# Order of score maxima, low parts of q and weight steps, PSUM bank order and idle matmuls in a fused attention and two-MLP kernel on one core

## The chip, the core and the metric

One Trainium2 chip, one of its cores. The metric is the device time of one execution in microseconds (us), the median of the runs shown. TensorE (PE) does the matmuls and has a queue of its own for weight loads (PEld); VectorE (DVE), ScalarE (ACT) and GpSimd (POOL) work on elements; SyncE's queue (SP) issues the DMAs. Each engine runs its own instructions in the order in which the program lists them, and waits on semaphores for what the others make.

## The reference

Batch 2, 12 heads, 448 positions, head size 64, all float32. Cut to what matters:

```python
scores = (q @ k.T) / 8                       # per head, 448 x 448
scores = where(upper triangle, -1e9, scores) # causal
p = exp(scores - max(scores))
attn = p / (sum(p) + 1e-9)
x = (attn @ v) -> 896 tokens x 768
y = (sigmoid(x @ w_gate) * (x @ w_val)) @ w_out        # d_ff 1536
h = y @ w_in                                           # 1024
s = h * softmax(h)
out = (layernorm(s) * g_ln) @ w_out2                   # 896 x 768
```

## The kernel before, in words

**Numbers.** A float32 operand of a matmul is split in two: a *high* part, which is the operand rounded to the type that PE takes, and a *low* part, which is what is left. A product is three matmuls: high by high, high by low, low by high (`TERMS`). So each operand costs two instructions outside PE, the low part after the high part. The weights come from memory as 64-bit words and are first turned into float32 by bit operations.

**Attention in pairs of heads.** The 24 heads are 12 pairs, `p` = 0 to 11. For one pair:

- q and k are loaded (`load_qk`, tile `qkr`); POOL makes k's and q's high parts (L223 and L236; for pair 0 DVE does it, since `prep_q_hi` is called with another engine there), DVE makes k's low part (`prep_k_lo`, L231) and q's low part (`prep_q_lo`, L253), all into one tile `qks`.
- The queries lie in four tiles of 64, 128, 128 and 128 rows that need 64, 192, 320 and 448 keys (`QE`). They are worked in two groups, `GROUPS` = tiles (3, 0) with 448 and 64 keys, and tiles (2, 1) with 320 and 192. A group's scores, for both heads of the pair, share one tile `s` of two PSUM banks, from the pool `ps_s`, which holds two such tiles. PE first writes the mask with bf16 matmuls (`sc_mask`, L341), then adds the scores (`sc_dots`, L354): for each query tile three times two matmuls, q's high part by k's high part, q high by k low, q low by k high.
- DVE takes the maxima (`sc_max`, L368), one instruction for each query tile and both heads, into the small tile `sum0`, `sum1` or `sum2` (the pairs in turn); ACT takes the exponentials (`sc_exp`, L375) into the tile `p`, one instruction for each query tile and head, and adds up the row sums.
- The probabilities are transposed by PE, in two units for each head (`tr_mm`, L426, tile `t`, pool `ps_t`); ACT makes the high part (`tr_hi`, L433), DVE the low part (`tr_lo`, L231), both into a tile `pt`. PE multiplies with v (`pv_mm`, L458, tile `x`, pool `ps_x`); v's two parts are made by POOL (`prep_v_hi`, L223; `prep_v_lo`, L231).
- The row sums' reciprocals (`recips`, L384) are spread by POOL and PE (`rs_wide`, `rs_mm`), copied by ACT (`rs_out`), and DVE multiplies the result (`x_mul`, L464). `x_hi` and `x_lo` split it for the next stage.

**The order.** It is written out by hand: a software pipeline of steps `s`, eight to a pair (`PER`). The table `STEPS` (L504) says for each function at which step, counted from the pair's own start at step 8p, it is issued, on which engine, and for which pairs (two further numbers, from and below). At each step the loop (L533) issues what is due, first on PE, then ACT, DVE, POOL; on one engine the order within a step is that of the table, and for a function with a negative step it is done ahead of the pair's start. So a row `(-8, 'D', prep_q_lo, 2)` puts q's low part of pairs from 2 on at the step at which the pair before starts. SP's queue holds the loads, issued where `prep_k_lo`, `prep_v_lo` and the weights' steps stand; pair 2's q and k are loaded behind pair 0's low parts.

**Idle matmuls.** `keep_warm` (L317, matmuls at L319, tile `warm`) issues bf16 matmuls whose result nobody reads: 56 at the front, 24 each at steps 2, 5 and 9.

**The weights' first chunks.** From step 88 the loop also prepares chunks of the first MLP's weights, one chunk `c` after another: an ACT scaling (L114) and three DVE steps (L117, L119, L122, the last one also issues the next chunk's load), then the high part on ACT (`chunk_hi`, L133) and the low part on DVE (`chunk_lo`, L136). Behind pair 11's start PE takes matmuls of the first MLP (`gv`) between the attention's (`early_tiles`, L478, matmuls at L490), in a PSUM tile of the pool `ps_s`; ACT copies them out (`pre`, L495).

**The next stages.** Then all PSUM banks go to one pool, and PE runs the first MLP's `gv` (L597), `pm` (L627), the second MLP's `h` (L657) and `po` (L718). A tile of the new pool waits for what last used its bank. The attention's pools take their banks in the order in which they are opened: `ps_s` the lowest four, then `ps_t` two, then `ps_x` two.

## Time and profile before

| | |
|---|---|
| median of 3 runs | 508.43 us (508.19 to 508.91) |
| the profiled execution | 507.66 us, its span 505.9 us |
| PE busy | 494.8 us, 98% of the span |
| DVE, ACT, POOL busy | 334.2, 224.5, 119.8 us (66%, 44%, 24%) |
| granted PE clock | 1.00 over the span |

The span runs from the first instruction to the last; the execution's own time also holds what lies around it. The attention takes about the first 122 us, the first MLP the time to some 378 us, the second one the rest. Two other facts help with the rows further below: "L354" is line 354 of the kernel before, and a bracket such as [1.30 <-DVE pt L231] gives the idle time of the engine just before the instruction, and the instruction that ended it. A row with a count, as x12, is a run of alike instructions and gives the start of the first and the time from it to the end of the last.

### The profile page before, as it was taken

Reading aid. Unit: us, or ns where it says so; the run is one execution under the profiler, and the core shown is the slowest. Engines: PE = TensorE matmul, PEld = TensorE weight load, DVE = VectorE, ACT = ScalarE, POOL = GpSimd, SP = SyncE. Lnnn points to the kernel's source line nnn. Section 1 sums busy time; section 2 is a strip of 40 time slices with the busy share of each in tenths; the row PEclk is TensorE's granted clock in tenths of the full one; section 3 lists DMA queues with packets and bytes.
Section 4 is the critical chain, followed back from the end, with each engine's and each line's share of the span. In section 5 each row is a group of like instructions: output and inputs, shape, how many; then the busy total and the mean of one; then the engine's idle time right before and its main releaser. Section 6 shows DMA issues by size and latency. Waiting matters only on the chain.

```text
span 505.9 us, 7924 instructions
## 1 busy us (share of the span) xinstructions
PE 494.8 (98%) x3076; PEld 455.0 (90%) x3076; DVE 334.2 (66%) x514; ACT 224.5 (44%) x481; POOL 119.8 (24%) x207
## 2 busy tenths in 40 slices
PE   8899999999999999999999999999999999999997
PEld 8789998988999999999999999999998888899997
DVE  6778787886576677778877676776664787831110
ACT  4687878765424434543454333334313242422211
POOL 4667676641000000000000000000060597710000
PEclk9999999999999999999999999999999999999999
DMA  5724242023323433454443323335530311000101
GB/s 152 235 64 104 69 109 65 23 64 125 112 76 126 134 127 118 163 166 128 164 166 122 134 100 131 113 132 166 183 129 0 123 66 63 1 32 34 60 32 62
DMA packets 13205, 52.81 MB, mean 104 GB/s; under 512 B 1776, under 2 KB 2288, under 8 KB 13168
## 3 DMA queue, kind: packets, MB, share of 16 engines
q1 hardware_dynamic: 13168, 52.31, 31.7%
q8 instruction: 24, 0.39, 0.3%
q14 instruction: 13, 0.11, 0.1%
HBM read 49.55 MB, written 2.75 MB: 103 GB/s over the span
## 4 chain that ended last, share of the span: by engine, by line
PE 78%; ACT 11%; DVE 6%; issue 2%; DMA 1%; POOL 0%; SPq 0%; DVEq 0%; POOLq 0%; ACTq 0%
PE gv L597 33%; PE pm L627 17%; PE po L718 12%; PE h L657 12%; ACT p L375 7%; ACT pt L433 3%; DVE sum L368 2%; DVE qks L253 2%; PE gv L490 2%; DMA qkr<-in_qk_dram 1%; PE tp L700 1%; PE x L458 1%; DVE pt L231 1%; PE t L426 1%; DVE rs L384 0%
## 5 line engine op out<-in xcount | busy, mean ns | idle before, releaser
L597 PE MATMUL gv<-xy,hl 128*128 128x448 f32 x828 | 168.1, 365 | 0.6 <-ACT pre L495 0.6
L597 PEld LDWEIGHTS gv<-xy,hl 128*128 128x128 f32 x828 | 155.4, 188 | 13.3 <-ACT pre L495 1.0
L627 PE MATMUL pm<-g,hl 128*128 128x448 f32 x432 | 87.7, 365 | 0.0
L627 PEld LDWEIGHTS pm<-g,hl 128*128 128x128 f32 x432 | 81.1, 188 | 6.4
L644 POOL TENSOR_SCALAR t<-t,g_sb 128x768 f32<-128x768 f32 x8 | 8.8, 1102 | 249.1 <-PE pm L627 248.1
L136 DVE TENSOR_TENSOR hl<-t,hl 128x768 fp32r<-128x768 f32 x36 | 34.8, 967 | 41.3 <-ACT hl L133 39.6
L718 PE MATMUL po<-wo,lt 128*128 128x384 f32 x336 | 60.6, 339 | 0.0
L657 PE MATMUL h<-wi,xy 128*128 128x512 f32 x252 | 59.2, 395 | 0.0
L718 PEld LDWEIGHTS po<-wo,lt 128*128 128x128 f32 x336 | 58.7, 188 | 0.1
L657 PEld LDWEIGHTS h<-wi,xy 128*128 128x128 f32 x252 | 47.2, 187 | 11.4
L375 ACT ACTIVATE p<-s,sum 128x448 f32<-128x448 f32 (+3 forms) x96 | 45.9, 499 | 25.2 <-DVE rs L384 17.8
L122 DVE SCALAR_TENSOR_TENSOR t<-raw,t 128x768 int32<-128x768 int32 (+1 forms) x56 | 53.0, 946 | 1.7
L119 DVE SCALAR_TENSOR_TENSOR t<-raw,t 128x768 int32<-128x768 int32 (+1 forms) x56 | 52.8, 943 | 1.8
L114 ACT ACTIVATE raw<-raw 128x768 f32<-128x768 f32 (+1 forms) x56 | 47.9, 865 | 10.6 <-DMA raw<-in_wo_dram 7.9
L458 PE MATMUL x<-pt,v 128*128 128x320 f32 (+3 forms) x252 | 51.1, 323 | 0.0
L231 DVE TENSOR_TENSOR pt<-t,pt 128x512 fp32r<-128x512 f32 (+1 forms) x48 | 32.3, 672 | 19.2 <-ACT pt L433 19.2
L458 PEld LDWEIGHTS x<-pt,v 128*128 128x128 f32 x252 | 38.9, 190 | 1.9
L117 DVE TENSOR_SCALAR t<-raw 128x768 int32<-128x768 int32 (+1 forms) x56 | 30.9, 552 | 4.7 <-ACT raw L114 4.7
L173 DVE TENSOR_TENSOR lt<-tp,lt 128x512 fp32r<-128x512 f32 x14 | 9.7, 690 | 36.4 <-ACT lt L172 36.4
L133 ACT CAST hl<-t 128x768 fp32r<-128x768 f32 x36 | 30.0, 832 | 4.8 <-PE pm L627 4.2
L368 DVE TENSOR_REDUCE sum<-s 128x2 f32<-128x896 f32 (+3 forms) x48 | 30.2, 668 | 2.0 <-PE s L354 2.0
L181 ACT ACTIVATE wk<-gv 128x448 f32<-128x448 f32 x23 | 11.3, 542 | 44.2 <-PE gv L597 44.2
(95 smaller groups left out, 550.9 us busy)
## 6 DMA issues: line engine op xcount, KB each, us to landing
raw<-in_gv_dram SPq DMA_DIRECT2D x24, 768.0 KB, 4.5
raw<-in_wo_dram SPq DMA_DIRECT2D x20, 768.0 KB, 4.5
raw<-in_wi_dram SPq DMA_DIRECT2D x12, 512.0 KB, 3.5
qkr<-in_qk_dram SPq DMA_DIRECT2D x22, 224.0 KB, 3.8
vr<-in_v_dram SPq DMA_DIRECT2D x12, 256.0 KB, 2.8
out_dram<-o SPq DMA_DIRECT2D x6, 384.0 KB, 2.3
qkr<-in_qk_dram SPq DMA_DIRECT2D x4, 112.0 KB, 2.7
out_dram<-o SPq DMA_DIRECT2D x2, 192.0 KB, 1.9
```

Source lines behind the costliest of these rows:

```text
L114: nc.scalar.activation(out=w1.bitcast(F32), in_=w1.bitcast(F32), func=AF.Copy, scale=2.0 ** -112)
L119: nc.vector.scalar_tensor_tensor(out=tt, in0=w1, scalar=-2 ** 31, in1=tt, op0=ALU.bitwise_and, op1=ALU.bitwise_or)
L122: nc.vector.scalar_tensor_tensor(out=tt, in0=w0, scalar=29, in1=tt, op0=ALU.logical_shift_right, op1=ALU.bitwise_or)
L136: nc.vector.tensor_tensor(out=lo, in0=t_t.pop(it), in1=f32(hi), op=ALU.subtract)
L231: (nc.gpsimd if eng == 'P' else nc.vector).tensor_tensor(out=out, in0=a, in1=b, op=ALU.subtract)
L368: nc.vector.reduce_max(out=sum_t[p % 3][:, 8 + 2 * i:10 + 2 * i], in_=ps_sc[p, i], axis=AX.X, negate=True)
L375: nc.scalar.activation(out=p_t[(2 * p + e) % NPB][:, POFF[i]:POFF[i] + n], in_=ps[:, 1 - e], func=AF.Exp, bias=mx, scale=1.0, accum_out=sm)
L458: nc.tensor.matmul(out=ps[:, 128 * j:], lhsT=l, rhs=pt_t[h][:, c, u, c0:c0 + S - 128 * j], start=(chunk == 0 and n == 0), stop=(chunk == 7 ...
L597: nc.tensor.matmul(out=ps[i, b], lhsT=w[:, a, cs], rhs=xy[kk][:, x, b * S:(b + 1) * S], start=(kk == 0 and a == 0 and x == 0), stop=(kk == ...
L627: nc.tensor.matmul(out=ps[b], lhsT=w[:, a, cs], rhs=g_t[kk][:, x, b * S:(b + 1) * S], start=(kk == 0 and a == 0 and x == 0), stop=(kk == N ...
L657: nc.tensor.matmul(out=h[:, n * 512:(n + 1) * 512], lhsT=xy[kk][:, a, tk], rhs=wi[n * NK + kk][:, c], start=(kk == 0 and i == 0), stop=(kk ...
L718: nc.tensor.matmul(out=ps[n], lhsT=lts[k // 4][:, a, k % 4], rhs=wo[k][:, c, cs], start=(k == 0 and i == 0), stop=(k == NF2 - 1 and i == 2))
```

## The change

It consists of six edits, and none alters what is computed.

1. The PSUM pools are opened in another order: `ps_t` has the lowest two banks, `ps_x` the next two, `ps_s` the highest four.
2. Idle matmuls: 44 instead of 56 at the front; instead of 24 each at steps 2, 5 and 9, there are 20 at step 8 and 8 at step 9.
3. For pair 0, group 0, the maxima are four instructions, one for each head and query tile, head by head, and the exponentials of both query tiles are issued in one step, head by head too.
4. Pair 0's scores of both groups are issued at step 0 (group 1's were at step 4), and its maxima of group 1 at step 1. Pair 1 keeps its groups at steps 0 and 4.
5. q's low part moves: for pair 1 from step -2 to step -5, ahead of k's low part; for pairs from 2 on from step -8 to step -7. At step -8 it was issued ahead of the maxima of group 0 of the pair before, at step -7 it stands behind them.
6. The weights' chunks take 8 steps each instead of 9, and within a chunk the steps stand at 0, 3, 5 and 7 (before 0, 2, 4 and 6), ahead of the high part at 8 and the low part at 9 (before 7 and 8).

```diff
--- before.py
+++ after.py
@@ -196,9 +196,9 @@
         ptp = actx.enter_context(tc.tile_pool(name="ptp", bufs=4, side="right"))
         st = actx.enter_context(tc.tile_pool(name="st", bufs=2, side="right"))
         xfp = actx.enter_context(tc.tile_pool(name="xfp", bufs=2, side="right"))
-        ps_s = actx.enter_context(tc.tile_pool(name="ps_s", bufs=2, space=PSUM, reuse_waits="tile"))
         ps_t = actx.enter_context(tc.tile_pool(name="ps_t", bufs=2, space=PSUM, reuse_waits="tile"))
         ps_x = actx.enter_context(tc.tile_pool(name="ps_x", bufs=2, space=PSUM, reuse_waits="tile"))
+        ps_s = actx.enter_context(tc.tile_pool(name="ps_s", bufs=2, space=PSUM, reuse_waits="tile"))
 
         NH = B * H
         qk_raw, qk_sp = {}, {}
@@ -318,7 +318,7 @@
             for _ in range(n):
                 nc.tensor.matmul(out=ps[:, :128], lhsT=identb, rhs=identb, start=True, stop=True)
 
-        keep_warm(56)
+        keep_warm(44)
         prep_k_hi(0)
         prep_k_lo(0)
         prep_q_hi(0, 'D')
@@ -364,16 +364,22 @@
             return sum_t[p % 3][:, k:k + 1], sum_t[p % 3][:, m:m + 1]
 
         def sc_max(p, g):
-            for i in GROUPS[g]:
-                nc.vector.reduce_max(out=sum_t[p % 3][:, 8 + 2 * i:10 + 2 * i], in_=ps_sc[p, i], axis=AX.X, negate=True)
-
-        def sc_exp(p, i):
-            n = QE[i]
-            ps = ps_sc.pop((p, i))
-            for e in range(2):
+            if p == 0 and g == 0:
+                for e in range(2):
+                    for i in GROUPS[g]:
+                        nc.vector.reduce_max(out=sums_of(p, i, e)[1], in_=ps_sc[p, i][:, 1 - e], axis=AX.X, negate=True)
+            else:
+                for i in GROUPS[g]:
+                    nc.vector.reduce_max(out=sum_t[p % 3][:, 8 + 2 * i:10 + 2 * i], in_=ps_sc[p, i], axis=AX.X,
+                                         negate=True)
+
+        def sc_exp(p, *tiles):
+            for e, i in ([(e, i) for e in range(2) for i in tiles] if p == 0 else
+                         [(e, i) for i in tiles for e in range(2)]):
+                n = QE[i]
                 sm, mx = sums_of(p, i, e)
-                nc.scalar.activation(out=p_t[(2 * p + e) % NPB][:, POFF[i]:POFF[i] + n], in_=ps[:, 1 - e], func=AF.Exp,
-                                     bias=mx, scale=1.0, accum_out=sm)
+                nc.scalar.activation(out=p_t[(2 * p + e) % NPB][:, POFF[i]:POFF[i] + n], in_=ps_sc[p, i][:, 1 - e],
+                                     func=AF.Exp, bias=mx, scale=1.0, accum_out=sm)
 
         def sums(p):
             rs = rs_t[p] = st.tile([128, 16], F32, tag="rs", name="rs")
@@ -500,26 +506,25 @@
         early = early_tiles()
         left = NE * 6 * NK
 
-        ONE = 2
         STEPS = (
-            (0, 'E', lambda p: sc_mm(p, (0, 1) if p >= ONE else (0,))),
-            (4, 'E', lambda p: sc_mm(p, () if p >= ONE else (1,))),
+            (0, 'E', lambda p: sc_mm(p, (0,) if p == 1 else (0, 1))), (4, 'E', lambda p: sc_mm(p, (1,)), 1, 2),
             *((s0 + d, eng, lambda p, f=f, u=u, a=a: f(2 * p + a, u))
               for u, a, s0 in ((1, 0, 9), (1, 1, 11), (0, 0, 13), (0, 1, 15))
               for d, eng, f in ((0, 'E', tr_mm), (1, 'A', tr_hi), (1 if s0 == 15 else 2, 'D', tr_lo))),
             *((13 + n, 'E', lambda p, n=n: pv_mm(p, n)) for n in range(len(CHUNKS))),
             (15, 'E', rs_mm),
-            (-7, 'P', prep_k_hi, 0, 2), (-6, 'P', prep_q_hi, 0, 2), (-2, 'D', prep_q_lo, 0, 2),
+            (-7, 'P', prep_k_hi, 0, 2), (-6, 'P', prep_q_hi, 0, 2), (-5, 'D', prep_q_lo, 0, 2),
             (-5, 'D', prep_k_lo, 0, 2),
-            (-10, 'P', prep_k_hi, 2), (-9, 'P', prep_q_hi, 2), (-8, 'D', prep_q_lo, 2), (-2, 'D', prep_k_lo, 2),
+            (-10, 'P', prep_k_hi, 2), (-9, 'P', prep_q_hi, 2), (-7, 'D', prep_q_lo, 2), (-2, 'D', prep_k_lo, 2),
             (3, ENG['lk'], last_keys), (7, ENG['vh'], prep_v_hi), (9, ENG['vl'], prep_v_lo),
             (8, 'P', sums), (9, 'D', recips), (10, ENG['rx'], rs_wide), (16, ENG['rr'], rs_out),
             (21, 'D', x_mul), (24, ENG['xh'], x_hi, 0, NPR - 1), (25, ENG['xl'], x_lo, 0, NPR - 1),
             (22, ENG['xh'], x_hi, NPR - 1), (23, ENG['xl'], x_lo, NPR - 1),
-            (1, 'A', lambda p: sc_exp(p, 3)), (2, 'A', lambda p: sc_exp(p, 0)),
+            (1, 'A', lambda p: sc_exp(p, 3, 0), 0, 1), (1, 'A', lambda p: sc_exp(p, 3), 1),
+            (2, 'A', lambda p: sc_exp(p, 0), 1),
             (5, 'A', lambda p: sc_exp(p, 2)), (6, 'A', lambda p: sc_exp(p, 1)),
-            (0, 'D', lambda p: sc_max(p, 0)),
-            (2, 'D', lambda p: sc_max(p, 1), ONE), (4, 'D', lambda p: sc_max(p, 1), 0, ONE),
+            (0, 'D', lambda p: sc_max(p, 0)), (1, 'D', lambda p: sc_max(p, 1), 0, 1),
+            (4, 'D', lambda p: sc_max(p, 1), 1, 2), (2, 'D', lambda p: sc_max(p, 1), 2),
         )
 
         def steps(s, eng):
@@ -531,8 +536,8 @@
 
 
         for s in range(PER * NPR + 26):
-            if s in (2, 5, 9):
-                keep_warm(24)
+            if s in (8, 9):
+                keep_warm(20 if s == 8 else 8)
             steps(s, 'E')
             for _ in range(2):
                 if s >= PER * NPR and left and next(early):
@@ -544,15 +549,16 @@
                 dma_next()
 
             for c in range(2 * NE + 2):
-                e = s - 88 - 9 * c
+                e = s - 88 - 8 * c
+                if e in (3, 5, 7):
+                    next(bits_now)
+                if e == 8 and c < 2 * NE:
+                    chunk_hi(c)
+                if e == 9 and c < 2 * NE:
+                    chunk_lo(c)
                 if e == 0:
                     bits_now = bits_steps(c)
-                if e in (0, 2, 4, 6):
                     next(bits_now)
-                if e == 7 and c < 2 * NE:
-                    chunk_hi(c)
-                if e == 8 and c < 2 * NE:
-                    chunk_lo(c)
         while left:
             left -= next(early)
         for t in range(NE):
```

In the diffs of the order below, names carry the number of their buffer, `out<-in`; the line numbers of the changed kernel are higher by up to 6.

**DVE, the first two pairs.** In DVE's list from the low part of pair 0's q on, before: `s_249` and `s_308` are pair 0's two groups of scores, `s_365` is pair 1's first, `qks_274` is pair 1's q and k, `qks_360` pair 2's.

```order
L253 SCALAR_TENSOR_TENSOR qks_241<-qkr_110,qks_241 128x448
L368 TENSOR_REDUCE sum0_157<-s_249 128x2 x2
L231 TENSOR_TENSOR qks_274<-qkr_115,qks_274 128x448
L368 TENSOR_REDUCE sum0_157<-s_308 128x2 x2
L253 SCALAR_TENSOR_TENSOR qks_274<-qkr_115,qks_274 128x448
L253 SCALAR_TENSOR_TENSOR qks_360<-qkr_246,qks_360 128x448
L368 TENSOR_REDUCE sum1_158<-s_365 128x2 x2
L384 RECIPROCAL rs_389<-rs_389 128x8
```

And now (`s_237` and `s_258` pair 0's scores, `s_327` pair 1's first, `qks_289` pair 1's, `qks_302` pair 2's):

```order
L253 SCALAR_TENSOR_TENSOR qks_229<-qkr_110,qks_229 128x448
L370 TENSOR_REDUCE sum0_157<-s_237 128x1 x4
L373 TENSOR_REDUCE sum0_157<-s_258 128x2 x2
L253 SCALAR_TENSOR_TENSOR qks_289<-qkr_115,qks_289 128x448
L231 TENSOR_TENSOR qks_289<-qkr_115,qks_289 128x448
L373 TENSOR_REDUCE sum1_158<-s_327 128x2 x2
L253 SCALAR_TENSOR_TENSOR qks_302<-qkr_234,qks_302 128x448
L390 RECIPROCAL rs_350<-rs_350 128x8
```

Pair 0's two groups of maxima now follow each other, and pair 1's first maxima stand ahead of pair 2's q low part, where they stood behind it.

**DVE, a later pair.** One pair's turn from one transposes' low part to the next, before (`s_649` and `s_670` are the pair's two groups, `qks_629` the next pair's q and k):

```order
L231 TENSOR_TENSOR pt_603<-t_631,pt_603 128x512
L253 SCALAR_TENSOR_TENSOR qks_629<-qkr_489,qks_629 128x448
L368 TENSOR_REDUCE sum0_157<-s_649 128x2 x2
L384 RECIPROCAL rs_702<-rs_702 128x8
L368 TENSOR_REDUCE sum0_157<-s_670 128x2 x2
L231 TENSOR_TENSOR pt_720<-t_704,pt_720 128x512
```

And now, with `s_595` and `s_616` in their places and `qks_575` as the next pair's:

```order
L231 TENSOR_TENSOR pt_549<-t_577,pt_549 128x512
L373 TENSOR_REDUCE sum0_157<-s_595 128x2 x2
L253 SCALAR_TENSOR_TENSOR qks_575<-qkr_435,qks_575 128x448
L390 RECIPROCAL rs_647<-rs_647 128x8
L373 TENSOR_REDUCE sum0_157<-s_616 128x2 x2
L231 TENSOR_TENSOR pt_666<-t_649,pt_666 128x512
```

q's low part has moved from ahead of the first group's maxima to behind them, and stays ahead of the reciprocals and of the second group's maxima.

**DVE, the last pair.** From the last maxima on, before (`raw_391` is the first chunk of weights):

```order
L368 TENSOR_REDUCE sum2_159<-s_1773 128x2 x2
L117 TENSOR_SCALAR t_1830<-raw_391 128x768
L231 TENSOR_TENSOR pt_1822<-t_1807,pt_1822 128x512
L119 SCALAR_TENSOR_TENSOR t_1830<-raw_391,t_1830 128x768
L231 TENSOR_TENSOR pt_1846<-t_1832,pt_1846 128x512
L464 TENSOR_TENSOR xf_1861<-x_1719,rb_1798 128x448
L122 SCALAR_TENSOR_TENSOR t_1830<-raw_391,t_1830 128x768
L231 TENSOR_TENSOR pt_1822<-t_1849,pt_1822 128x448
```

And now (`raw_352` is the first chunk):

```order
L373 TENSOR_REDUCE sum2_159<-s_1719 128x2 x2
L231 TENSOR_TENSOR pt_1768<-t_1753,pt_1768 128x512
L117 TENSOR_SCALAR t_1786<-raw_352 128x768
L231 TENSOR_TENSOR pt_1792<-t_1776,pt_1792 128x512
L470 TENSOR_TENSOR xf_1806<-x_1665,rb_1744 128x448
L119 SCALAR_TENSOR_TENSOR t_1786<-raw_352,t_1786 128x768
L231 TENSOR_TENSOR pt_1768<-t_1794,pt_1768 128x448
L122 SCALAR_TENSOR_TENSOR t_1786<-raw_352,t_1786 128x768
```

Each step of the first chunk of weights has moved behind the transposes' low part that it stood ahead of.

## Rows read from the trace of the kernel before

**Rows 1.** The chain that ended last, its shares of the span by engine.

```profile
PE 78%; ACT 11%; DVE 6%; issue 2%; DMA 1%; POOL 0%; SPq 0%; DVEq 0%; POOLq 0%; ACTq 0%
```

**Rows 2.** Windows: length, busy us of PE, PEld, DVE, ACT, POOL, PEclk, DMA, GB/s.

```profile
10.00:20.00 10.00, 8.23 (x114) 7.49 (x113) 7.05 (x12) 6.72 (x29) 6.59 (x14) 1.00 0.65 230
...
130.00:290.00 160.00, 160.00 (x791) 148.28 (x790) 116.60 (x162) 66.59 (x103) 0.00 (x0) 1.00 0.39 131
```

**Rows 3.** PE's waits over the span: what for, us, times, longest.

```profile
PE t L426 <- DVE pt L231: 4.5, 12, 1.3
...
PE gv L597 <- ACT pre L495: 0.6, 1, 0.6
PE gv L490 <- DVE hl L136: 0.6, 1, 0.6
```

**Rows 4.** The chain that ended last, near the start: start us, us, what.

```profile
6.01 0.64 DVE qks L253
7.22 4.42 DMA qkr<-in_qk_dram
...
12.38 0.54 POOL qks L236
12.94 0.91 DVE qks L253
13.85 1.21 DVE sum L368 x2
```

**Rows 5.** PE's timeline: start us, us from first to last, engine, line, instruction.

```profile
1.61 4.68 PE L319 MATMUL warm<-identb 128*128 128x128 bf16 x56 [1.61 <-DVE identb L280]
...
7.44 1.51 PE L319 MATMUL warm<-identb 128*128 128x128 bf16 x24
...
11.65 1.11 PE L354 MATMUL s<-qks 64*128 64x448 f32 x12
...
17.74 0.33 PE L426 MATMUL t<-identx,p 128*128 128x128 f32 x1 [1.30 <-DVE pt L231]
...
19.62 0.30 PE L426 MATMUL t<-identx,p 128*128 128x128 f32 x1 [0.47 <-DVE pt L231]
...
27.15 0.33 PE L426 MATMUL t<-identx,p 128*128 128x128 f32 x1 [0.58 <-DVE pt L231]
...
88.75 1.11 PE L354 MATMUL s<-qks 64*128 64x448 f32 x12
...
104.08 0.33 PE L426 MATMUL t<-identx,p 128*128 128x128 f32 x1 [0.39 <-DVE pt L231]
```

**Rows 6.** Groups by form, 0 to 110 us: count, busy us, mean ns, idle before.

```profile
L368 DVE TENSOR_REDUCE sum<-s 128x2 f32<-128x896 f32 x12 | 12.9, 1079 | 1.2 <-PE s L354 1.2
...
L368 DVE TENSOR_REDUCE sum<-s 128x2 f32<-128x128 f32 x12 | 3.3, 275 | 0.0
```

**Rows 7.** DVE's timeline, columns as in rows 5.

```profile
7.55 1.29 DVE L368 TENSOR_REDUCE sum<-s 128x2 f32<-128x896 f32 x2 [0.92 <-PE s L354]
...
11.34 0.61 DVE L253 SCALAR_TENSOR_TENSOR qks<-qkr,qks 128x448 fp32r<-128x448 f32 x1
...
89.53 0.79 DVE L253 SCALAR_TENSOR_TENSOR qks<-qkr,qks 128x448 fp32r<-128x448 f32 x1
...
91.56 1.23 DVE L368 TENSOR_REDUCE sum<-s 128x2 f32<-128x640 f32 x2
...
93.49 0.69 DVE L231 TENSOR_TENSOR pt<-t,pt 128x512 fp32r<-128x512 f32 x1 [0.70 <-ACT pt L433]
...
102.14 1.27 DVE L119 SCALAR_TENSOR_TENSOR t<-raw,t 128x768 int32<-128x768 int32 x1
```

**Rows 8.** ACT's timeline, columns as in rows 5.

```profile
8.94 0.63 ACT L375 ACTIVATE p<-s,sum 128x448 f32<-128x448 f32 x1 [4.10 <-DVE sum L368]
...
10.46 0.32 ACT L375 ACTIVATE p<-s,sum 128x64 f32<-128x64 f32 x1
```

**Rows 9.** POOL's timeline, columns as in rows 5.

```profile
14.43 1.42 POOL L231 TENSOR_TENSOR v<-vr,v 128x384 fp32r<-128x384 f32 x2
```

## The prediction

> **What bounds the kernel now.** I read the page first, there the chain that ended last: PE holds 78% of it, ACT 11% and DVE 6% [rows 1]. So a saving counts only where PE waits. The windows say where that is: PE is busy 8.23 of the ten microseconds from 10 to 20 us, but 160.00 of 160 us from 130 to 290 us [rows 2]. The list of PE's waits then adds up all there is to win after the start: twelve waits for the low part of the transposed probabilities, 4.5 us in all, and two single waits of 0.6 us, for the weights' low part and for the copy `pre` [rows 3].
>
> Which work is late there is told by the chain [rows 4]. It comes from the load of pair 2's q and k, which takes until 11.64 us, through POOL's high parts and DVE's low part of q of pair 2 (12.94 us, 0.91 us), and only then do pair 1's maxima run (13.85 us). Pair 1's maxima do not need pair 2's q. They stand behind it in DVE's order, although PE had pair 1's first scores finished at 12.76 us (11.65 + 1.11) [rows 5]. From the maxima the chain goes through the exponentials to a transpose that PE starts at 17.74 us after 1.30 us of idleness; the next such wait is 0.47 us, pair 1's is 0.58 us, and one near the end 0.39 us [rows 5]. That leaves 4.5 - 1.30 - 0.47 - 0.58 - 0.39 = 1.76 us for the other eight, 0.22 us for each later pair.
>
> **The change, part by part.** All sums are against the profiled execution (span 505.9 us, its own time 507.66 us, 0.77 us under the median of 508.43 us); I carry the difference over to the median.
>
> *Start (pairs 0 and 1).* Idle matmuls: 24 take 1.51 us, 0.063 us each; the first 56 take 4.68 us, 1.15 us more than at that rate [rows 5], as if some of them ran at the lower level (1.2 GHz). Twelve fewer end the front 0.76 us earlier, at 5.5 us (1.61 + 4.68 - 0.76). Pair 0's first dots then wait for q's high part, which DVE ends just ahead of q's low part, and the third pair of matmuls waits for the low part, done at 6.65 us (6.01 + 0.64) [rows 4]; eight matmuls at the pace of the 1.11 us burst [rows 5] end at about 7.3 us, 0.2 us earlier than before.
>
> The maxima of group 0 become four reductions over one head each. None is in the trace. From the forms of 896 and 128 elements, 1.079 and 0.275 us [rows 6], one element costs 1.05 ns and an instruction 0.14 us: 0.61 us for 448, 0.21 us for 64. With the 0.07 us by which neighbours overlap, four take 1.43 us where two took 1.29 us [rows 7]. Bounds: 1.29 us (work by element alone) and 1.8 us (no overlap, and 64 elements as long as 128: 2 x (0.61 + 0.275)). I take the fit, and the maxima end at 8.76 us. Splitting them frees nothing early: the first exponential waits for all four, since they write one tile.
>
> The four exponentials took 8.94 to 10.78 us [rows 8], so now end at 10.70 us. That frees the score tile for pair 1's masks, at 10.75 us. DVE meanwhile does group 1's maxima (1.23 us), then pair 1's q low and k low (0.61 us each) [rows 7], from 8.7 until 11.1 us with the hand-overs. The third dot of pair 1 waits for that, and some 0.85 of the 1.11 us burst follows: 11.95 us. Pair 1's maxima start at 12.0 instead of 13.78 us, because pair 2's q low part (ready for POOL's sake at 12.92 us) now comes after them. **Term: -1.8 us**, between -1.4 (reductions at 1.8 us) and -2.1 us (the burst without a hitch). Exponentials, high part, low part and the transpose shift with it; the waits of 1.30 and 0.47 us stay, as they are part of that chain. Next to be late is v's low part, which POOL ends at 15.85 us (14.43 + 1.42) [rows 9]; PE would reach its first use at some 16.5 us, so it just stays hidden. The 44 other idle matmuls that vanish (2.8 us) lie in stretches where PE would wait anyway, so I cost them at nothing beyond this shift; that is true while masks wait for the exponentials.
>
> *Steady pairs.* Each period had 0.79 us of q's low part ahead of the maxima [rows 7]. It now stands between the two groups' maxima, beside ACT's exponentials of group 0. In the period that I read, q low ended at 90.32 us (89.53 + 0.79) and the maxima followed, while PE's dots of group 0 had ended at 89.86 us (88.75 + 1.11) [rows 5, 7]: they may start 0.46 us earlier. PE's wait is 0.22 us, so it goes. What is late next: between the maxima of group 0 and the transposes' low part DVE now has q low (0.61 us) besides group 1's maxima (1.23 us). There it sat idle 0.70 us until ACT was done [rows 7], and 0.61 us of that is now used. **Term: -0.58 - 1.76 = -2.3 us**, between 0 and -2.3 us.
>
> *Drain.* The first weights' steps run one step later: the short shift instead of the 1.27 us step stands ahead of a transpose's low part, so the wait of 0.39 us at 104.08 us [rows 5, 7] goes. The wait for the weights' low part (0.6 us) turns into one for the high part, which is now made later too: 0, with bounds -0.6 and +0.4 us. The other wait of 0.6 us [rows 3] ends because the transposes' banks are lowest: the first `gv` tile of the next stage then takes a bank that is long free, not the one that `pre` is copied from. **Term: -1.0 us**, between -0.6 and -1.6 us. Chunks 2 and 3 get their steps earlier by up to three steps, on engines that are then idle: 0.
>
> **Sum:** -1.8 - 2.3 - 1.0 = -5.1 us; 507.66 becomes 502.6 us, and the median 508.43 becomes **503.3 us**. With all bounds: -2.0 to -6.0 us, so 502.4 to 506.4 us. The steady bound of 0 is a case of its own, below; with the steady term kept the ends are 502.4 and 504.1 us.
>
> **Rivals.**
> 1. *The steady wait stays.* The moved q low part delays group 1's maxima and with them the transposes' low part. For it: only some 0.1 us of the 0.70 us idle time is left, and the same instruction takes 0.61 us at 11.34 us but 0.91 us at 12.94 us, where POOL works too [rows 4, 7]; at 0.91 us the margin is gone. Against it: POOL waits for the reciprocal behind it, so it runs alone. Then -1.8 - 1.0 = -2.8 us: 505.6 us, and 504.5 us if half the wait stays. The Trainium skill ("SBUF — State Buffer", Who interferes with whom) says that a VectorE instruction with two inputs in SBUF and a reading GpSimd instruction block each other for a whole instruction; by that rule a meeting would cost 0.54 us, one POOL instruction [rows 4]. The row at 12.94 us shows 0.30 us lost, so the trace agrees in kind and shows less.
> 2. *The clock falls, and the kernel is slower.* PE's granted clock is 1.00 (2.4 GHz) in all rows [rows 2], also across the pause of 1.30 us. The change takes out 56 idle matmuls and leaves longer pauses before pair 1's masks and before the first transpose (15.95 us). At 1.2 GHz PE's work takes twice as long, and the front's extra 1.15 us is what one return cost: one fall gives 504.5 us. Slower than before by 0.2% needs over 6.1 us lost, 12 us at the lower level, so six falls, or a low level through pairs 1 and 2. Against it: longer idle time with little change in busy share did not lower it before. The Trainium skill ("TensorE: Matmul & The Clock Gate", What's actually happening) says that the half rate is the default and that only activity keeps the clock up, which speaks against taking idle matmuls out; by that rule a fall costs what is priced here, and no row of this kernel shows one after the start.
> 3. *The start's shift is lost* to POOL: v's low part or pair 2's preparation, both bound by the load until 11.64 us [rows 4], hold the first product chunk, and about 1 us of the 1.8 goes: 504.3 us.
>
> **How the numbers follow.** Forecast 503.3 us (502.4 to 504.1): 0.66. Rival 1: 0.16. Rival 3: 0.08. Rival 2: 0.07, of which 0.03 ends slower than 509.4 us. Several gains being larger than rows say (overlap in the dots, the drain's -1.6 us): 0.03. Timings of this kernel spread over 0.7 us, so about 0.2% (1.0 us) can be told from no change. Faster 0.94, same 0.03, slower 0.03. The range 502.0 to 505.7 us takes in the forecast, rivals 1 and 3 and one fall of the clock; outside lie a fall that lasts and gains well beyond all bounds.
>
> **What would show it.** In the new profile pair 1's maxima start near 12.0 us, with pair 2's q low part after them; pair 2's score masks stand some 1.8 us earlier; PE's list of waits keeps about 1.3 and 0.5 us for the transposes and none of 0.2 us in later pairs; the first `gv` matmuls of the next stage follow without a wait, some 5 us earlier than now. I am wrong if the small waits come back with DVE named, if idle matmuls lie 0.11 us apart after 5 us, or if PE waits for POOL's v.

## The result, and the profile after

The changed kernel takes **501.65 us** (median of 4 runs, 501.51 to 501.92) against 508.31 us before (4 runs, 508.09 to 508.91): a ratio of 0.9868, 95% interval 0.9851 to 0.9885, so 6.7 us less. The direction was forecast. The size was not: 503.3 us was expected, and 501.65 us lies 0.35 us below the range. The profiled execution took 501.62 us, its span is 499.7 us (before 505.9 us).

The page of the profile after shows in its chain, by engine, that PE now holds nearly all of the path (78% in [rows 1]):

```profile
PE 94%; DVE 2%; ACT 2%; issue 1%; POOL 0%; POOLq 0%; DVEq 0%; ACTq 0%
```

The list of PE's waits after (what for, us in total, times, longest), beside [rows 3]:

```profile
PE t L432 <- DVE pt L231: 1.7, 2, 1.2
...
PE s L341 <- ACT p L381: 1.3, 1, 1.3
PE gv L496 <- ACT hl L133: 1.0, 1, 1.0
PE gv L496 <- ACT pre L501: 0.2, 1, 0.2
```

Ten of the twelve waits for the transposes' low part are gone, and so is the one at the entry of the next stage. New is a wait of pair 1's masks for pair 0's exponentials, in a place where idle matmuls ran before.

Where the 6.2 us of span went is read from the places at which PE starts a pair's masks or a stage. PE's timeline before (start us, us, engine, line, instruction), at the first masks of pair 2, of pair 11, and at the next stage:

```profile
21.12 0.23 PE L341 MATMUL s<-maskb,identb 64*128 64x128 bf16 x2
...
96.95 0.23 PE L341 MATMUL s<-maskb,identb 64*128 64x128 bf16 x2
...
122.92 12.43 PE L597 MATMUL gv<-xy,hl 128*128 128x448 f32 x60 [0.62 <-ACT pre L495]
```

And PE's timeline after, with the waits between:

```profile
5.75 0.23 PE L341 MATMUL s<-maskb,identb 64*128 64x128 bf16 x2
...
10.81 0.23 PE L341 MATMUL s<-maskb,identb 64*128 64x128 bf16 x2 [1.27 <-ACT p L381]
...
10.98 1.12 PE L354 MATMUL s<-qks 64*128 64x448 f32 x12
...
16.11 0.33 PE L432 MATMUL t<-identx,p 128*128 128x128 f32 x1 [1.23 <-DVE pt L231]
...
18.00 0.30 PE L432 MATMUL t<-identx,p 128*128 128x128 f32 x1 [0.47 <-DVE pt L231]
...
19.49 0.23 PE L341 MATMUL s<-maskb,identb 64*128 64x128 bf16 x2
...
91.80 0.23 PE L341 MATMUL s<-maskb,identb 64*128 64x128 bf16 x2
...
102.85 0.68 PE L496 MATMUL gv<-xy,hl 128*128 128x448 f32 x2 [0.95 <-ACT hl L133]
...
116.77 18.40 PE L603 MATMUL gv<-xy,hl 128*128 128x448 f32 x90
```

| stretch | before, us | after, us | difference | forecast |
|---|---|---|---|---|
| to pair 2's masks | 21.12 | 19.49 | -1.63 | -1.8 |
| pair 2's to pair 11's masks | 75.83 | 72.31 | -3.52 | -2.3 |
| pair 11's masks to the next stage | 25.97 | 24.97 | -1.00 | -1.0 |
| from there to the end of the span | 382.98 | 382.93 | -0.05 | 0 |

Start and drain came as forecast; the later pairs gained 1.2 us more. One such pair shows why. PE before, from six matmuls with v to a transpose that waited, and on to one that did not:

```profile
92.92 1.11 PE L458 MATMUL x<-pt,v 128*128 128x448 f32 x6
94.24 0.33 PE L426 MATMUL t<-identx,p 128*128 128x128 f32 x1 [0.21 <-DVE pt L231]
...
94.65 1.00 PE L458 MATMUL x<-pt,v 128*128 128x320 f32 x6
95.49 0.27 PE L426 MATMUL t<-identx,p 128*128 128x128 f32 x1
```

The same first two groups after:

```profile
88.11 1.11 PE L464 MATMUL x<-pt,v 128*128 128x448 f32 x6
89.09 0.33 PE L432 MATMUL t<-identx,p 128*128 128x128 f32 x1
```

The transpose that waited started 1.32 us after the six matmuls began, now it is 0.98 us: 0.34 us less, for a wait whose row says 0.21 us. The row counts from the *end* of the last matmul, which the profile models. In an unbroken stream the next matmul starts before that end: 95.49 us is 0.16 us ahead of 95.65 (94.65 + 1.00), and 89.09 is 0.13 us ahead of 89.22. So a wait cost its row and this lost overlap.

DVE's timeline after shows the moved instruction where the diff put it, behind the maxima, and the low part of the transposes behind it without a wait (before: 0.70 us of idle time, [rows 7]):

```profile
12.13 1.29 DVE L373 TENSOR_REDUCE sum<-s 128x2 f32<-128x896 f32 x2 [1.14 <-PE s L354]
13.34 0.81 DVE L253 SCALAR_TENSOR_TENSOR qks<-qkr,qks 128x448 fp32r<-128x448 f32 x1
...
86.30 0.75 DVE L253 SCALAR_TENSOR_TENSOR qks<-qkr,qks 128x448 fp32r<-128x448 f32 x1
86.97 0.19 DVE L390 RECIPROCAL rs<-rs 128x8 f32<-128x8 f32 x1
87.08 1.23 DVE L373 TENSOR_REDUCE sum<-s 128x2 f32<-128x640 f32 x2
88.35 0.69 DVE L231 TENSOR_TENSOR pt<-t,pt 128x512 fp32r<-128x512 f32 x1
```

### The profile page after: what moved, and what is told of

Its sections match the earlier page's. It is cut to its first block, busy times and chain, and to the rows that moved or that the text cites. A ratio compares the mean times of both kernels' runs of the same rounds, so it can differ in the third digit from the quotient of the medians.

```text
span 499.7 us, 7812 instructions
## 1 busy us (share of the span) xinstructions
PE 490.5 (98%) x3020; PEld 452.4 (91%) x3020; DVE 333.7 (67%) x516; ACT 224.7 (45%) x481; POOL 117.6 (24%) x207
## 4 chain that ended last, share of the span: by engine, by line
PE 94%; DVE 2%; ACT 2%; issue 1%; POOL 0%; POOLq 0%; DVEq 0%; ACTq 0%
PE gv L603 34%; PE pm L633 18%; PE po L724 12%; PE h L663 12%; PE x L464 6%; PE t L432 4%; PE s L354 4%; PE gv L496 1%; PE tp L706 1%; PE s L341 1%; PE r L404 1%; PE warm L319 1%; ACT p L381 1%; DVE pt L231 1%; DVE sum L373 0%
## 5 line engine op out<-in xcount | busy, mean ns | idle before, releaser
L373 DVE TENSOR_REDUCE sum<-s 128x2 f32<-128x640 f32 (+3 forms) x46 | 29.0, 672 | 3.6 <-PE s L354 3.6
```

## The experiments

Three theories stood against each other for the later pairs. **A:** the order of q's low part is the whole gain, and a wait costs its row and 0.13 us. **B:** a wait costs its row, the rest is another edit's. **C:** the banks carry it. The runs of the kernel before beside the experiments had medians of 508.07 to 508.41 us.

**e1, q's low part put back** in the changed kernel, pairs 3 to 11:

```diff
-(-7, 'D', prep_q_lo, 2)
+(-7, 'D', prep_q_lo, 2, 3), (-8, 'D', prep_q_lo, 3)
```

> The changed kernel (501.65 us, period of a later pair 8.03 us), with q's low part of pairs 3 to 11 put back ahead of the maxima of the pair before. Theory A: the order of q's low part is the whole gain of the later pairs, and a wait of PE costs its row and 0.13 us more, because the matmul ahead of it is no longer overlapped by the next. Then nine waits on the transposes' low part come back (about 0.5 and eight of 0.22 us), the period is 8.39 us again, and the time is 501.65 + 3.5 = 505.2 us. Theory B: a wait costs what its row shows, and the rest of the gain of the later pairs is from another edit. Then the same rows come back, but the period is 8.25 us and the time 504.0 us. Theory C: another edit (the banks) carries the later pairs. Then the period stays 8.03 us and the time 501.7 us.

505.39 us (504.96 to 505.81), ratio 0.9945 (0.993 to 0.996). PE's timeline, one period from masks to masks:

```profile
61.90 0.19 PE L341 MATMUL s<-maskb,identb 64*128 64x64 bf16 x2
...
67.45 0.33 PE L432 MATMUL t<-identx,p 128*128 128x128 f32 x1 [0.22 <-DVE pt L231]
...
70.29 0.19 PE L341 MATMUL s<-maskb,identb 64*128 64x64 bf16 x2
```

The period is 8.39 us and the row 0.22 us: 0.36 us more for 0.22 us shown. That is theory A, and B and C fall.

**e2, q's low part moved alone** in the kernel before, for pairs 3 to 11; pair 2's stays at -8.

```diff
-(-8, 'D', prep_q_lo, 2)
+(-8, 'D', prep_q_lo, 2, 3), (-7, 'D', prep_q_lo, 3)
```

> The kernel before (508.31 us, period 8.39 us), with q's low part of pairs 3 to 11 alone moved behind the maxima of the pair before; pair 2's stays where it was, and so does all else. Theory A: the period falls to 8.03 us, the nine waits after pair 2's first masks go, and the time is 508.31 - 3.5 = 504.8 us. Theory B: the waits go, the period falls to 8.17 us only, and the time is 506.0 us. Theory C: the period stays 8.39 us and the time 508.3 us.

504.57 us (504.53 to 504.62), 3.5 us under the 508.07 us beside it; ratio 0.9929 (0.9914 to 0.9944). The old banks, the old idle matmuls and the old weights' steps all stand in it. Of the waits on the transposes' low part only the two of the start and the last pair's (0.38 us) are left, and the period is 8.04 us:

```profile
45.77 0.19 PE L341 MATMUL s<-maskb,identb 64*128 64x64 bf16 x2
...
53.81 0.19 PE L341 MATMUL s<-maskb,identb 64*128 64x64 bf16 x2
```

One moved instruction is more than half of the whole gain.

**e12, q's low part twice** in its new place, to find the margin and price a longer wait:

```diff
 (-7, 'D', prep_q_lo, 2),
+(-7, 'D', prep_q_lo, 3),
```

> The changed kernel with q's low part of pairs 3 to 11 computed twice in its new place, one after the other, with the same result. The transposes' low part behind it ended 0.05 us before PE took its bank in the later pairs, so there is no margin: the period grows by the time of one more instruction, 0.54 to 0.7 us, and the time by nine times that, 501.65 + 4.9 to 6.3 us = 506.5 to 508 us. Theory A: PE's row of this wait is 0.13 us shorter than what the period grew by. Theory B: the row is as long as what the period grew by. Third reading: there was a margin of 0.3 us or more, and the period grows by less than 0.3 us, 504.4 us or less.

506.23 us (505.19 to 507.05), ratio 0.9955 (0.9936 to 0.9974).

```profile
53.92 0.19 PE L341 MATMUL s<-maskb,identb 64*128 64x64 bf16 x2
...
59.52 0.33 PE L432 MATMUL t<-identx,p 128*128 128x128 f32 x1 [0.27 <-DVE pt L231]
...
62.36 0.19 PE L341 MATMUL s<-maskb,identb 64*128 64x64 bf16 x2
```

The period grew by 0.41 us (8.44), the row shows 0.27: again 0.14 us more than the row. The second instruction adds about 0.54 us (half of the pair's 1.27 us, less the 0.1 us by which neighbours overlap), so the margin was some 0.13 us, larger than expected here. One of the nine periods is longer: there the two instructions took 1.79 us, the row shows 0.79 us and the period is 8.96 us, 0.93 us more, which is the row and 0.14 us once more.

**e5, the whole move of q's low part** in the kernel before, pairs 1 and 2 too:

```diff
-(-2, 'D', prep_q_lo, 0, 2)
+(-5, 'D', prep_q_lo, 0, 2)
-(-8, 'D', prep_q_lo, 2)
+(-7, 'D', prep_q_lo, 2)
```

> The kernel before with the whole move of q's low part (pair 1's to step -5, pairs from 2 on to step -7), and nothing else of the change. Theory A: besides the 3.5 us of the later pairs, pair 1's maxima now wait for PE's scores alone and start at 12.8 instead of 13.78 us; the start gains 1.0 us, the other 0.65 us of the 1.63 us being the burst's and the idle matmuls'. Time 508.31 - 3.5 - 1.0 = 503.8 us, pair 2's masks at 20.1 us. Rival: the start's gain needs the earlier scores of pair 0, and this gives the later pairs' gain alone, 504.8 us. Other rival: the move is the whole gain of the start, 503.2 us, pair 2's masks at 19.5 us.

503.6 us (503.12 to 504.01), 4.7 us under the 508.28 us beside it, ratio 0.9911 (0.9895 to 0.9928). Pair 1's maxima start at 12.66 us and pair 2's masks at 20.02 us, 1.10 us earlier than before (0.14 us of that may be the front's, which ended earlier in this execution). So the order on DVE is some 1.0 us of the start's 1.63 us, as expected.

**e11, pair 0's scores, maxima and exponentials as before** in the changed kernel:

```diff
-(1, 'A', lambda p: sc_exp(p, 3, 0), 0, 1), (1, 'A', lambda p: sc_exp(p, 3), 1),
-(2, 'A', lambda p: sc_exp(p, 0), 1),
+(1, 'A', lambda p: sc_exp(p, 3)), (2, 'A', lambda p: sc_exp(p, 0)),
...
-(0, 'D', lambda p: sc_max(p, 0)), (1, 'D', lambda p: sc_max(p, 1), 0, 1),
-(4, 'D', lambda p: sc_max(p, 1), 1, 2)
+(0, 'D', lambda p: sc_max(p, 0)), (4, 'D', lambda p: sc_max(p, 1), 0, 2)
```

> The changed kernel with the edits of pair 0's scores, maxima and exponentials undone: two maxima over both heads, exponentials in two steps by query tile, group 1 at step 4; q's low part, idle matmuls, weights and banks as changed. On PE the order stays the same, as nothing stands between the two groups. Pair 1's low parts of q and k come ahead of pair 0's second maxima on DVE, so its dots run without a hitch and its first maxima start at about 11.9 instead of 12.13 us; pair 0's second exponentials start 0.2 to 0.4 us later, and with them pair 0's first transposes. Theory: these edits are worth next to nothing, 501.4 to 501.9 us. Rival: they carry what the start gained beyond the move of q's low part (0.5 to 0.65 us): 502.2 us.

502.1 us (501.78 to 502.48). The changed kernel itself, run again beside it (e10), had 502.15 us, and pair 2's masks stand at 19.62 and 19.56 us. The split of the maxima, the exponentials' order and the burst are worth nothing that can be measured.

**e6, the idle matmuls of before** in the changed kernel:

```diff
-keep_warm(44)
+keep_warm(56)
...
-if s in (8, 9):
-    keep_warm(20 if s == 8 else 8)
+if s in (2, 5, 9):
+    keep_warm(24)
```

> The changed kernel with the idle matmuls of the kernel before: 56 at the front, 24 each at steps 2, 5 and 9. The front ends 0.75 us later, and with 48 idle matmuls (3.0 us) behind pair 0's scores pair 1's masks stand behind the idle matmuls instead of waiting 1.27 us. Theory A: pair 1's masks move from 10.81 to about 11.3 us, pair 2's by as much, and the time is 502.2 us, without any run above 502.7 us, since PE has no pause there before the transposes. Rival: idle matmuls cost nothing here, since all else hides them: 501.7 us. Other rival: the front is what counts, 0.75 us: 502.4 us.

502.87 us (502.39 to 503.25). Pair 2's masks come at 20.73 us, 1.24 us later than in the changed kernel. More than expected, since the front ended 1.2 us later (first masks at 6.98 us): in this execution the granted clock first rose at 6.12 us, after 4.96 us in the profile of the changed kernel, so the 1.24 us are not the edit's alone. Pair 1's masks (12.03 us) stand right behind 48 idle matmuls (9.24 us + 2.85 us). In e11, whose clock rose nearly as late (5.99 us) but whose idle matmuls are the changed kernel's, they come at 10.95 us and pair 2's at 19.62 us: against that, 1.1 us are the idle matmuls'. With an early rise (e5) only about 0.5 us of the start's gain are left for them, and that by exclusion, since the other edits gave nothing there. So their worth hangs on when the clock rises.

**e3, the old banks** in the changed kernel:

```diff
+ps_s = ... "ps_s" ...
 ps_t = ... "ps_t" ...
 ps_x = ... "ps_x" ...
-ps_s = ... "ps_s" ...
```

> The changed kernel with the PSUM pools opened in the old order (scores lowest). Theory A: the later pairs keep 8.03 us; only the first matmul of the next stage waits again for the copy out of the early tile, 0.62 us by its row before and 0.13 us for the overlap lost: 502.4 us. Theory C: the period is 8.25 to 8.39 us, and the time 504 to 505 us. A third reading, that the early weights or the copy are there in time without the banks: no wait and 501.7 us.

Ten runs, 502.82 to 509.14 us, median 508.21: three at 502.8 to 503.2 us, one at 504.1, six at 508.1 us or more. Pair 2's to pair 11's periods are 8.03 to 8.04 us from pair 3 on, so C falls once more. The entry of the next stage costs 0.76 us more (25.61 us from pair 11's 64-row masks, after 24.85), as theory A has it: a row of 0.62 us and the overlap. But the profiled execution, at 509.14 us, shows two things that no theory had. The groups of PE by shape, first MLP, of e3:

```profile
L603 PE MATMUL gv<-xy,hl 128*128 128x448 f32 x828 | 171.4, 368 | 0.6 <-ACT pre L501 0.6
L633 PE MATMUL pm<-g,hl 128*128 128x448 f32 x432 | 89.4, 368 | 0.0
```

And of the changed kernel:

```profile
L603 PE MATMUL gv<-xy,hl 128*128 128x448 f32 x828 | 168.0, 366 | 0.0
L633 PE MATMUL pm<-g,hl 128*128 128x448 f32 x432 | 87.7, 366 | 0.0
```

The same 1260 matmuls run slower by 3.4 and 1.7 us at a granted clock of 1.00. And early on the clock falls (the mean granted clock of the execution is 0.996; 0.996 and 0.997 stand in two more of the ten runs, one of them the one of 504.1 us, so the fall and the longer time do not go together); a window of e3 (length, busy us of PE, PEld, DVE, ACT, POOL, PEclk, DMA, GB/s):

```profile
18.20:21.50 3.30, 3.30 (x22) 2.97 (x22) 1.75 (x3) 2.53 (x9) 2.67 (x5) 0.50 1.03 351
```

the same window of the changed kernel:

```profile
18.20:21.50 3.30, 3.30 (x50) 3.09 (x50) 2.40 (x4) 2.42 (x9) 2.75 (x6) 1.00 1.01 363
```

**e4, the old weights' steps** in the changed kernel (`e = s - 88 - 9 * c` with steps 0, 2, 4, 6, 7, 8).

> The changed kernel with the weights' steps in their old places (nine steps to a chunk; 0, 2, 4, 6, 7, 8). The prediction's reading: the wait of a transpose in the last pair comes back, 0.39 us and 0.13 us of lost overlap, while the wait of the first early matmul for the weights falls from 0.95 to about 0.6 us: +0.15 us, 501.8 us, so this edit alone is worth next to nothing. The rival: chunks 2 and 3, which come later again, are waited for by the next stage as well, and the time is 502.5 us or more.

502.17 us (501.86 to 503.25). The longest run is the profiled one, and it has the fall of the clock at 18 us too (pair 3's 64-row masks at 29.24 us, after 27.66). The drain, from pair 11's 64-row masks to the next stage, took 25.06 us, after 24.85: the steps' move is worth 0.2 us, as expected.

**e14, the new banks alone** in the kernel before.

> The kernel before with the new order of the banks and nothing else. The prediction's reading: the wait of 0.62 us for the copy out of the early tile goes, and with the overlap that it cost 0.75 us: 507.4 us; the later pairs keep 8.39 us and the list of waits its twelve on the transposes' low part. Rival: the copy, no longer waited for, delays the weights or the next early tile, and the time stays 508.2 us.

507.53 us (506.94 to 508.31, 10 runs), ratio 0.9985 (0.9976 to 0.9994) to the 508.41 us beside it: 0.9 us (0.3 to 1.2 by the interval), and the wait at the entry is gone: from pair 11's 64-row masks to the next stage it took 25.05 us, after 25.84. As expected. The first masks came 1.07 us later than in the profile before (7.29 after 6.22 us), pair 2's only 0.10 us later (21.22 us): before the change it was not PE's front that bound the start.

**e13, old banks and filled pauses, and e15, the weights' steps back as well:** where does the slower pace of e3 come from?

> The changed kernel with the old order of the banks and with idle matmuls in pair 1's pauses (as in the run that filled them). In the run with the old banks alone, the 828 and 432 matmuls of the first MLP followed each other every 206.7 ns instead of 202.7 ns, 5.0 us in all, and some of its runs stood at 503, others at 508 to 509 us. Reading F: the wait of 0.62 us at the stage's entry sets the slower pace in some executions, whatever the clock did before. Then the times fall into two groups again, about 502.5 and 507.5 us, and none of them 1.3 us higher. Reading G: the fall of the clock at 18 us is what brings it about; then, with the pauses filled, all runs are at 502.5 us.

Six runs: 502.48 to 503.41 us, and 508.31 us, which is the profiled one: 171.4 and 89.4 us for the two groups again, and no fall of the clock. So the slower pace does not need the fall of the clock: of the two readings in the expectation G is refuted, and F agrees.

> The kernel of the first of these three runs (old banks, pauses filled) with the weights' steps in their old places as well, so that the end of the attention is that of the kernel before, of which no run showed the slower pace. If the pace at the stage's entry hangs on what comes just ahead of it: all runs in one group at 502.3 + 0.6 = 502.9 us. If it hangs on the wait alone: two groups, 502.9 and 507.9 us.

502.66 to 503.8 us, 4 runs, one group. Four runs are few (one of e13's six was a slow one), so that the weights' steps matter is not shown. In all profiles the slower pace stood only in e3 and e13, which have both the wait at the entry and the new weights' steps. Why the one wait brings it on and that of the kernel before does not was not found.

**e7, the pauses of pair 1 filled** in the changed kernel:

```diff
-if s in (8, 9):
-    keep_warm(20 if s == 8 else 8)
+if s in (8, 9, 13, 15):
+    keep_warm({8: 38, 9: 8, 13: 17, 15: 5}[s])
```

> The changed kernel with more idle matmuls in the pauses of pair 1: 38 at step 8 (20 before), 17 at step 13 and 5 at step 15, none of which PE has time to lose by: its waits of 1.27, 1.23 and 0.47 us shrink to about 0.15 us each. Theory D: the fall of the granted clock to 1.2 GHz at 18 us that the runs with the old banks and with the old weights' steps showed comes from the two pauses ahead of it, 1.23 and 0.47 us; then no run of this kernel shows it, all times are 501.4 to 502.0 us, and the profile has 1.00 throughout. Rival: the fall has another cause; then some runs are 1.3 us longer, at 503 us, and the clock's row shows an 8 in the second slice. Other rival: idle matmuls in these places delay the work behind them, 502.2 us in all runs.

502.0 us (501.49 to 502.42). No run at 503 us, and the waits shrank to 0.27, 0.17 and 0.17 us. But the spread is wider than expected, and D (that the fall comes from the two pauses ahead of it) is not proved: the profiled run, the longest, has the clock's first rise as late as 7.51 us, and PE's first scores ran at the lower level. The mean granted clock of every run speaks for D: none of the 23 runs with filled pauses (e7, e8, e9, e13, e15) is below 0.999, while six of the 31 with the pauses of the changed kernel (itself, e1, e3, e4, e10, e12) are at 0.995 to 0.997, where e3's and e4's profiles show the fall.

**e8, pair 0's first transposes evicted earlier**, on top of e7's filling:

```diff
-(1, 'A', tr_hi), (2, 'D', tr_lo)        # all pairs
+(0, 'A', tr_hi), (1, 'D', tr_lo)        # pair 0, first unit
```

> The kernel of the run before with pair 0's first transposes evicted one step earlier: ACT makes their high part ahead of pair 1's exponentials, at 13.2 us instead of 14.9 us, DVE the low part as soon as pair 2's q low part is done, 14.1 us instead of 15.37 us, and idle matmuls fewer (9 at step 13). The wait of 1.23 us at 16.11 us falls by what pair 1's exponentials allow: they start 0.5 us later, and so come later to the second low part. Theory: the chain through ACT is what holds PE there, and 0.5 us go: 501.1 us. Rival: the exponentials, now later, hold the next transposes instead, and the time stays 501.65 us. A gain of the full 1.23 us would be 500.4 us.

501.19 us (500.74 to 502.24). The wait at 16.11 us is gone from the list, and pair 2's masks stand 0.7 us earlier (18.89 us for the 64-row ones, after 19.61). It agrees with the first theory, though its runs overlap those of the changed kernel (501.51 to 501.92 us).

**e10, the changed kernel again, and e9, e8 with q's high part of pair 0 on ACT.**

> The changed kernel once more (one blank line added), as a control beside the next two. 501.65 us again. If the instant at which the granted clock first rises (4.3 to 7.5 us in the traces so far) sets the spread of the times, its profile has another front than 5.75 us for pair 0's masks, and the time differs by no more than 0.6 us; one run of several may show the fall of the clock at 18 us and come out at 503 us.

502.15 us (501.64 to 503.32): two of five runs stand above 503 us. The one of 503.13 us has a mean granted clock of 0.997, as e4's profiled run with the fall; the one of 503.32 us has 1.000 and a span of 500.8 us, so it is not the fall; about half of its excess over the profiled run (501.64 us, span 499.9 us) lies outside the span.

> The changed kernel with pair 0's first transposes evicted one step earlier and idle matmuls in the pauses, as in the earlier run of that (501.19 us), and with pair 0's q high part on ACT ahead of ACT's zero copies instead of on DVE between k's and q's low parts, and 38 idle matmuls at the front. DVE's q low part then ends some 0.4 us earlier (6.1 instead of 6.5 us) and pair 0's dots may start at 5.4 us instead of 5.98 us. Theory: DVE's three instructions for pair 0 set the front, 0.4 us go, 500.8 us. Rival: the first rise of the clock sets it, since fewer idle matmuls only move slow matmuls into the scores: 501.2 us as before.

501.12 us (500.74 to 501.64), ratio 0.9856 (0.9841 to 0.9872). The theory falls, for a reason that ACT's timeline of e9 gives:

```profile
5.37 0.58 ACT L236 ACTIVATE qks<-qkr 128x448 fp32r<-128x448 f32 x1 [3.15 <-DMA qkr<-in_qk_dram]
```

q's high part waits for its load until 5.37 us, so no engine could make it much earlier: DVE began it at 5.45 us in the changed kernel. In this profile the wait for the first transposes is back too (0.72 us at 16.34 us, pair 2's 64-row masks at 19.83 us), behind pair 2's q low part, which waited for POOL until 14.08 us: what e8 gains hangs on when pair 2's q is ready. As a version, e9 was 1.0 us below the changed kernel beside it, and none of its runs was above 501.7 us; the intervals (e10's is 0.9865 to 0.9899) overlap, so that it beats it is likely, not shown.

## Why the prediction was right or wrong

**What bounds the kernel: right.** Pair 1's maxima stood behind pair 2's q low part. Moving it gave 1.0 us of the start (e5) and 3.5 us of the later pairs (e1, e2); and a front 1.07 us later on PE moved pair 2's masks by 0.10 us only (e14).

**Start, -1.8 us forecast, -1.63 us measured.** Four maxima took 1.42 us (forecast 1.43), pair 1's masks came at 10.81 us (10.75), the dots ended at 12.10 us (11.95), the maxima started at 12.13 us (12.0). Waits of 1.23 and 0.47 us stayed, as said. That the split frees nothing held (e11). Of the 1.63 us some 1.0 us is the order on DVE (e5); the rest came with fewer idle matmuls ahead of pair 1's masks (e6, e11).

**Later pairs, -2.3 us forecast, -3.52 us measured: the step that failed.** The term was "-0.58 - 1.76 = -2.3 us, between 0 and -2.3 us": the sum of nine rows of PE's waits, which was taken for the most that there was to win ("adds up all there is to win after the start"). The mechanism held; this term was mis-sized. Each wait cost 0.35 us where its row says 0.21 or 0.22 us, and in e12 0.41 us where the row says 0.27 us, because the matmul ahead of a wait runs out without the next one overlapping it. Nine times 0.13 us are the missing 1.2 us, and rows of the kernel before showed it: the six matmuls that last 1.00 us at 94.65 us are followed after 0.84 us. That gains could be "larger than rows say" had a chance of 0.03.
The Trainium skill ("TensorE: Matmul & The Clock Gate", Single matmul latency and Back-to-back issue gap) tells a lone matmul's latency and the shorter distance of matmuls in a stream apart; from its two formulas for bf16 matmuls at the higher clock the difference would be about 0.16 us, an estimate, where the runs show 0.13 to 0.14 us.

**Drain, -1.0 us forecast, -1.00 us measured.** The wait at the entry was worth 0.76 us with its overlap (e3; 0.79 in e14's profile), where 0.6 us was forecast; the weights' steps 0.2 us (e4), where 0.39 us was, since the wait for the weights grew to 0.95 us, within the bound of +0.4 us that was given. That the sum agrees to the hundredth is luck: the two misses offset each other.

**From the profile to the median: failed as well.** The prediction carried the profiled execution's distance to the median over. That distance was 0.77 us before and is 0.03 us after, so 0.7 us of the miss of 1.65 us is this. The other 0.9 us is the profiled execution's, for which 502.6 us was forecast and 501.62 us measured: the 1.2 us of the later pairs, less the start's 0.17 us and some 0.1 us behind and outside the span.

**Rival 1, the wait stays: refuted.** The margin is thin, as said (some 0.1 us forecast, 0.13 us by e12), but it holds; q's low part took 0.75 us at 86.30 us, not alone as said (POOL's low part of x ran until 86.57 us), and did not delay PE. **Rival 2, the clock falls:** the forecast of 1.00 held in the profiled execution; a fall is real, though: seen in the profiles of e3 and e4, whose start is that of the changed kernel. It is not the change's alone: four of the 48 runs of the kernel before beside the experiments have a mean granted clock of 0.996 or 0.997 as well, where the prediction's rows showed no fall. In e4 it put pair 3's masks 1.6 us back (29.24 after 27.66); 1.15 us had been given for it. None of the falls came near the 6.1 us that would have made the kernel slower than before. **Rival 3** did not occur.

## What to carry to other kernels

In this kernel a wait in PE's list was worth its row plus the overlap that the break cost: compare start to start with the same pair of instructions where nothing waits, above all when many short waits are added up. Look first for an instruction that stands in an engine's order ahead of more urgent work that does not need its result; moving q's low part behind the maxima was 4.5 to 4.7 of the 6.7 us here. And where one wait stands ahead of a long uniform stage, run more than once: in e3 and e13 some executions with such a wait were 5 us longer, for a reason that was not found.

## What the runs showed of the hardware

**Two paces of the same matmuls.** From the stage's start to the next stage's, 828 matmuls of 448 columns took 167.8 us in the changed kernel (116.77 to 284.58), 202.7 ns each, and 171.2 us in e3 (119.17 to 290.39), 206.8 ns each, at a granted clock of 1.00 in both. Over the first MLP this is 5 us. The pace was kept for the stage, and by the times it differed between executions of one kernel (e3 and e13 fall into two groups 5 us apart).

**The first rise of the clock is not fixed to the program.** In the traces it came between 4.25 us (e5) and 7.51 us (e7) after the span's start, although PE began at 1.6 us each time. 56 idle matmuls took 4.54 us in e5 and 5.75 us in e14, where it came at 6.79 us. (The page's row of the clock shows 1.00 ahead of the first rise too; the idle matmuls tell the lower level: eight took 1.06 us from 4.78 us in e9, whose clock rose at 6.51 us, and 0.62 us from 12.15 us.) In e3 and e4, where the rise came at 4.5 us, the clock fell to 1.2 GHz at 18.1 us, after PE had been idle for 1.23 and 0.47 us, and was back at 21.5 us; in the changed kernel, with a rise at 4.96 us and the same pauses, it did not fall, nor in the kernel before, with a rise at 4.55 us and pauses of 1.30 and 0.47 us. What decides it is not shown.

**VectorE and GpSimd slow each other.** In the drain after, DVE's timeline and then POOL's:

```profile
100.32 1.60 DVE L122 SCALAR_TENSOR_TENSOR t<-raw,t 128x768 int32<-128x768 int32 x1
...
107.72 0.95 DVE L122 SCALAR_TENSOR_TENSOR t<-raw,t 128x768 int32<-128x768 int32 x1
```

```profile
84.03 1.43 POOL L231 TENSOR_TENSOR v<-vr,v 128x384 fp32r<-128x384 f32 x2
...
100.11 2.14 POOL L231 TENSOR_TENSOR v<-vr,v 128x384 fp32r<-128x384 f32 x2
```

Side by side the weights' step took 0.65 us longer than at 107.72 us, where POOL was idle, and v's low part 0.71 us longer than at 84.03 us, where DVE read one of its operands from PSUM. The weights' step ends at 101.92 us in the chain to the wait of 0.95 us (ACT makes the high part from 101.96 us, and PE goes on at 102.85 us), so this meeting may hold part of the drain's last gain; no run took it out.
